# A fused attention and ELU layer: the last block's last two projections batch by batch, and three moves of x given to ScalarE

## The chip, the core and the metric

The kernel runs on one core of one Trainium2 chip. The metric is device time in microseconds (us). Five engines work side by side, each in the order of its own instructions: TensorE (PE, with its weight loads as PEld), VectorE (DVE), ScalarE (ACT), GpSimd (POOL) and SyncE (SP), which here does nothing but issue DMAs. They wait for one another through semaphores.

## What is computed

A linear attention with a decaying state, and then a layer with an ELU between two matrices:

```python
# B, H, S, D = 4, 8, 768, 48 ; d_model = 384, d_ff = 2048
for t in range(S):
    cur = np.einsum('bhd,bhe->bhde', u[None] * kt, vt)
    y[:, :, t] = np.einsum('bhd,bhde->bhe', rt, state + cur)
    state = w[None, :, :, None] * state + np.einsum('bhd,bhe->bhde', kt, vt)
x = y.transpose(0, 2, 1, 3).reshape(B * S, H * D)
h = x @ w_in
g = np.where(h > 0.0, h, np.exp(np.minimum(h, 0.0)) - 1.0)
return g @ w_out
```

The inputs and the result are float32.

## The kernel before

The 768 time steps are cut into six blocks (n = 0 to 5) of 128. A pair (n, b), block and batch, is a unit. A unit's attention gives 128 tokens of x, and the four units of a block stand side by side in x[n], 512 columns wide, kept as a high and a low part whose sum is x (xh and xl), so that each product is made of three matrix products. The layer goes through d_ff in 16 slices (f = 0 to 15). For each (n, f):

- `hidden` (L1171): nine matmuls ps_h <- x, weights, 512 columns, one group of three for each of three 128-row parts c of x;
- `negative` (L1184, ACT, L1188 and L1189), `elu` (L1192, DVE, L1194), `split_g` (L1196: the high part by ACT at L1200, the low part by DVE at L1202);
- `project` (L1205): for each batch b three matmuls of 384 columns that add to ps_acc[b]; they need the two parts of g. It follows two steps behind `hidden`.

After slice 15, `store` (L1221) copies the four sums to `stage`, alternately by ACT (L1231) and DVE (L1229), and SP stores each at once (L1233). The last block has nothing behind it: `run` (L286) does both outstanding projections, f = 14 and f = 15, and then the store.

`fill_x` (L1086) completes x. A unit's eight heads come out as rows of x in four parts, each with 16 rows to spare in both halves, and the fourth part's rows are moved into these spare rows of the other three by six small DMAs, one for each half i and part c (L1098). It is done for batches 0 to 2 at once (384 columns, 48 KB each) and for batch 3 apart (128 columns, 16 KB each). Before block n's first `hidden` can multiply part c, the moves of c in both halves must have landed.

The order is written by hand. `step` (L393) goes through a list of names, `FIRST` for block 0 and `LATER` for the others, and each engine runs its instructions in the order in which they are written there. In `FIRST` the order of the names that matter here is: `hid`, `bk7` (ACT's copy of moved keys, L665, for the unit after), `neg`, `elu`, `gh`, `Gb`, `proj`. `Gb` is `fill_x`; for unit (1, 3) it falls into step (0, 15), the step before block 1's first `hidden`.

Of the kernel before, what the change touches and what calls it, by code (L numbers as in the profile page):

```python
# [17 lines left out]
P = 128  # L18
B, H, S, D = 4, 8, 768, 48
DP = 64  # L20
HP = H // 2
DM, DFF = 384, 2048
NC = DM // P
NF = DFF // P
NCH = S // P
# [8 lines left out]
FILLS = [slice(i * DP + D, (i + 1) * DP) for i in range(2)]  # L34
# [22 lines left out]
class Kernel:  # L57
# [180 lines left out]
    def run_general(self):  # L238
        self.u_by_tokens()
        self.powers_by_tokens()  # L240
        self.reverse_powers()
        self.level_tables()
        self.load_v(0, 1)
        self.load_weights(0)
        self.load_weights(1)
        for n in range(NCH):
            self.all_banks = n == 0
            for b in range(B):
                self.turn_in(n, b)
                self.decay_in(n, b)  # L250
                self.current(n, b)
                self.key_rest(n, b)
                self.scores_by_levels(n, b)
                self.outputs(n, b)
                self.new_state(n, b)
                self.load_after(n, b, self.load_rk)
                self.load_after(n, b, self.load_v)
                for i in range(2):
                    self.split_x(n, b, i)
                self.fill_x(n, b)  # L260
            self.all_banks = False
            for f in range(NF):
                if n == 0:
                    if f == 0:
                        for j in range(2, 2 * DEEP - 1):
                            self.load_weights(j)
                    for k in (0, 1) if f == 0 else (f + 1,):
                        self.widen(k)
                        self.low_bits(k)
                        self.merge(k)  # L270
                        self.sign(k)
                        for j in (2 * k + 2 * DEEP - 1, 2 * k + 2 * DEEP):
                            self.load_weights(j)
                        self.split_w(k)
                        for i in range(2):
                            self.rest_w(k, i)
                self.hidden(n, f)
                self.negative(n, f)
                self.elu(n, f)
                for i in range(2):  # L280
                    self.split_g(n, f, i)
                self.project(n, f)
                if f == NF - 1:
                    self.store(n)

    def run(self):  # L286
        self.start()
        for n in range(NCH):
            for f in range(NF):
                self.step(n, f)  # L290
        for f in (NF - 2, NF - 1):
            self.project(NCH - 1, f)
        self.store(NCH - 1)

    def start(self):
        nc = self.nc
# [96 lines left out]
    def step(self, n, f):  # L393
        nc = self.nc
# [5 lines left out]
        last = divmod(n * NF + f - (1 if (n, f) < EARLY else 2), NF)  # L400
# [49 lines left out]
            "elu": lambda: self.elu(n, f),  # L450
            "gh": lambda: self.split_g(n, f, 0),
            "gl": lambda: self.split_g(n, f, 1),
            "proj": lambda: self.project(*last) if last in self.g else None,
            "Lw": lambda: [self.load_weights(j) for j in (2 * k + 2 * DEEP - 1, 2 * k + 2 * DEEP) if n == 0],
            "wd": lambda: self.widen(k + 1),
            "lb": lambda: self.low_bits(k + 1),
# [14 lines left out]
        if (n, f) == (0, NF - 1):  # L471

            o = self.late.bitcast(F32).rearrange("p s d w -> p (s d w)")[:, 0 : B * DM]
# [612 lines left out]
    def fill_x(self, n, b):  # L1086

        if self.general:
            cols = slice(b * P, (b + 1) * P)
        elif b < HP - 2:  # L1090
            return
        else:
            cols = slice(0 if b == HP - 2 else b * P, (b + 1) * P)
        x = self.x[n].bitcast(F32)[:, :, :, cols]
        for i in range(2):
            for c in range(NC):
                rows = slice(i * DP + c * FILL, i * DP + (c + 1) * FILL)
                self.nc.sync.dma_start(x[FILLS[i], :, c], x[rows, :, NC])  # L1098


    def level_tables(self):
# [100 lines left out]
            nc.vector.tensor_sub(part, g, self.g[n, f][2].bitcast(F32))  # L1202
        self.g[n, f].append(part)

    def project(self, n, f):  # L1205
        gh, gl = self.g.pop((n, f))[2:]
        wh, wl = self.weight(f + 1, 0)
        if f == 0:
            self.acc[n] = [
                self.ps.tile([P, 512], F32, tag=f"acc{b}", name=f"ps_acc{b}", bufs=1)  # L1210
                for b in range(B)
            ]
        for b in range(B):
            at = slice(b * P, (b + 1) * P)
            for i, (a, w) in enumerate(((gh, wh), (gh, wl), (gl, wh))):
                self.nc.tensor.matmul(  # L1216
                    self.acc[n][b][:, 0:DM], lhsT=a[:, at], rhs=w,
                    start=(f == 0 and i == 0), stop=(f == NF - 1 and i == 2),
                )

    def store(self, n):  # L1221
        nc = self.nc
        for b, po in enumerate(self.acc.pop(n)):
            if self.general:
                o = self.wk.tile([P, DM], F32, tag="o", name="o", bufs=2)
            else:
                o = self.o[:, b, :]
            if b % 2:
                nc.vector.tensor_copy(o, po[:, 0:DM])  # L1229
            else:  # L1230
                nc.scalar.copy(o, po[:, 0:DM])  # L1231
            row = b * S + n * P
            nc.sync.dma_start(self.out[row : row + P, :], o)  # L1233
# [43 lines left out]
```

## Time and profile before

| what | us |
|---|---|
| median of 3 runs | 504.34 (504.28 to 504.58) |
| the profiled execution, whole | 505.23 |
| its span, first to last instruction | 503.5 |
| TensorE busy (matmuls) | 487.5, 97% of the span |
| VectorE, ScalarE, GpSimd busy | 284.8, 256.9, 153.6 |

Times within the span are counted from its start, in us. The profiled execution lies 1.73 us above its span and 0.89 us above the median. A row of the timeline gives start, length, engine, line, operation, and in brackets how long the engine stood idle before it and what ended that; "SPq" is a DMA issue on SP's queue. The granted clock (PEclk) is a share of TensorE's full 2.4 GHz.

### The profile page before, as it was taken

To read this page: it belongs to the slowest core of one execution; us is meant where nothing else is said; L and a number is where in the kernel's file an instruction comes from. 1 tells how busy PE (TensorE), PEld (TensorE's weight loads), DVE (VectorE), ACT (ScalarE), POOL (GpSimd) and SP (SyncE) were. 2 spreads that over 40 slices of the span, in tenths; PEclk is the share of its full clock that TensorE was granted. 3 is DMA by queue.
4 is the path that set the end of the run, shared out by engine and by line. 5 is a ranking of instruction groups with operands and counts; after the bars stand their busy time and mean duration, and the time that the engine had idled before them with its cause. 6 is when DMAs were issued, how large, how long until landed. Compare 5 with 4: busy or idle time off the path is not lost.

```text
span 503.5 us, 11963 instructions
## 1 busy us (share of the span) xinstructions
PE 487.5 (97%) x4890; PEld 430.2 (85%) x4890; DVE 284.8 (57%) x501; ACT 256.9 (51%) x449; POOL 153.6 (31%) x169
## 2 busy tenths in 40 slices
PE   8989999999999999999999999999999999999995
PEld 6888887977988988889888888888888989999995
DVE  6989899894565454554454654653654533433331
ACT  2468888863543544544444445445535435444442
POOL 4466769663331322312312303313212201000000
PEclk9999999999999999999999999999999999999999
DMA  9987796834624524624533524444333120100001
GB/s 157 230 184 164 197 182 171 158 92 113 164 61 90 138 61 98 176 61 90 120 79 91 162 61 96 106 77 112 103 108 101 45 65 10 62 1 1 1 0 69
DMA packets 102276, 51.08 MB, mean 101 GB/s; under 512 B 78786, under 2 KB 98116, under 8 KB 102212
## 3 DMA queue, kind: packets, MB, share of 16 engines
q1 hardware_dynamic: 102212, 50.22, 41.7%
q8 instruction: 40, 0.66, 0.6%
q14 instruction: 24, 0.20, 0.2%
HBM read 35.13 MB, written 13.11 MB: 96 GB/s over the span
## 4 chain that ended last, share of the span: by engine, by line
PE 74%; POOL 8%; ACT 4%; DVE 4%; issue 3%; DMA 3%; SPq 1%; ACTq 0%; POOLq 0%; DVEq 0%
PE ps_acc L1216 33%; PE ps_h L1179 32%; POOL wl L612 4%; PE ps_y L985 2%; PE ps_a L907 2%; PE ps_y L993 2%; PE ps_a L921 1%; POOL k_t L735 1%; DMA x<-x 1%; PE ps_y L855 1%; ACT g L1189 1%; ACT g L1188 1%; DMA stage<-in_moe_w_in_dram 1%; ACT x_f L1004 1%; SPq L1098 1%
## 5 line engine op out<-in xcount | busy, mean ns | idle before, releaser
L1216 PE MATMUL ps_acc<-wh,g 128*128 128x384 f32 x768 | 217.0, 343 | 0.4 <-DVE stage L1229 0.2
L1179 PE MATMUL ps_h<-x,wh 128*128 128x512 f32 (+1 forms) x588 | 180.3, 388 | 1.3 <-DMA x<-x 1.3
L1216 PEld LDWEIGHTS ps_acc<-wh,g 128*128 128x128 f32 x768 | 140.1, 188 | 6.2 <-DVE stage L1229 1.3
L1216 PE MATMUL ps_acc<-wl,g 128*128 128x384 f32 x384 | 129.2, 336 | 0.0
L1194 DVE SCALAR_TENSOR_TENSOR ps_h<-g,ps_h 128x512 f32<-128x512 f32 x96 | 66.7, 694 | 103.1 <-ACT g L1189 103.0
L1179 PEld LDWEIGHTS ps_h<-x,wh 128*128 128x128 f32 x588 | 108.1, 188 | 18.2 <-DMA x<-x 1.4
L1179 PE MATMUL ps_h<-x,wl 128*128 128x512 f32 (+1 forms) x294 | 114.8, 391 | 2.6 <-POOL wl L612 2.6
L1188 ACT ACTIVATE g<-ps_h 128x512 f32<-128x512 f32 x96 | 57.6, 600 | 87.5 <-PE ps_h L1179 87.5
L1200 ACT CAST g<-ps_h 128x512 fp32r<-128x512 f32 x96 | 56.3, 587 | 74.6 <-DVE ps_h L1194 74.1
L1202 DVE TENSOR_TENSOR g<-ps_h,g 128x512 fp32r<-128x512 f32 x96 | 66.2, 689 | 45.1 <-ACT g L1200 44.6
L1216 PEld LDWEIGHTS ps_acc<-wl,g 128*128 128x128 f32 x384 | 72.1, 188 | 2.1
L1179 PEld LDWEIGHTS ps_h<-x,wl 128*128 128x128 f32 x294 | 55.2, 188 | 16.0 <-POOL wl L612 4.7
L1189 ACT ACTIVATE g<-g 128x512 f32<-128x512 f32 x96 | 60.7, 632 | 3.1
L735 POOL TENSOR_TENSOR k_t<-k_t,rev 128x384 f32<-128x384 f32 x22 | 24.7, 1123 | 99.4 <-DVE ru L717 92.9
L1022 POOL TENSOR_TENSOR x<-x_f,x 128x512 fp32r<-128x512 f32 x16 | 20.7, 1297 | 90.0 <-ACT x L1020 84.7
L612 POOL TENSOR_TENSOR wl<-wide,wh 128x384 fp32r<-128x384 f32 x29 | 35.9, 1258 | 16.6 <-ACT wh L605 16.6
L969 DVE COPY_PREDICATED a<-mask,ps_a 128x256 f32<-128x256 int32 x40 | 17.7, 444 | 32.3 <-PE ps_a L921 32.3
L1004 ACT COPY x_f<-ps_y 128x256 f32<-128x256 f32 x40 | 12.9, 375 | 43.7 <-PE ps_y L993 43.7
L656 POOL TENSOR_TENSOR rk<-rk,pw 128x512 f32<-128x512 f32 x16 | 19.0, 1190 | 42.2 <-DMA rk<-blocks 42.2
L962 POOL TENSOR_TENSOR a<-ident_h,diag 128x512 f32<-128x512 f32 x20 | 21.6, 1079 | 6.7 <-DVE diag L728 5.3
L1013 DVE TENSOR_TENSOR x_f<-x_f,ps_y 128x128 f32<-128x128 f32 x40 | 9.7, 283 | 22.2 <-ACT x_f L1004 22.2
L587 DVE SCALAR_TENSOR_TENSOR wide<-stage 128x768 int32<-128x768 int32 (+1 forms) x17 | 21.1, 1239 | 0.0
(122 smaller groups left out, 411.0 us busy)
## 6 DMA issues: line engine op xcount, KB each, us to landing
blocks<-tb SPq DMA_DIRECT2D x64, 128.0 KB, 2.3
rk<-blocks SPq DMA_DIRECT2D x16, 512.0 KB, 3.5
stage<-in_moe_w_out_dram SPq DMA_DIRECT2D x16, 384.0 KB, 4.4
stage<-in_moe_w_in_dram SPq DMA_DIRECT2D x32, 144.0 KB, 4.2
out_dram<-stage SPq DMA_DIRECT2D x24, 192.0 KB, 4.2
r_t<-in_r_dram SPq DMA_DIRECT2D x22, 192.0 KB, 4.2
k_t<-in_k_dram SPq DMA_DIRECT2D x22, 192.0 KB, 3.2
v_t<-in_v_dram SPq DMA_DIRECT2D x22, 192.0 KB, 4.9
```

The source lines that it names most:

```text
L587: self.nc.vector.scalar_tensor_tensor(self.place(self.wide, k, WIDE), high, 3, low, op0=ALU.logical_shift_left, op1=ALU.bitwise_or,)
L612: (eng or self.nc.gpsimd).tensor_sub(lo, a, hi.bitcast(F32))
L735: (eng or self.nc.gpsimd).tensor_mul(k, k, self.rev[:, :, 0:D])
L962: self.nc.gpsimd.tensor_mul(un["a"], self.ident_h.unsqueeze(1).to_broadcast([P, H, DP]), un["diag"].unsqueeze(2).to_broadcast([P, H, DP]),)
L1022: (eng or nc.gpsimd).tensor_sub(x[:, 1], xf, x[:, 0].bitcast(F32))
L1179: self.nc.tensor.matmul(ph[:, part], lhsT=a[:, c * P : (c + 1) * P], rhs=x[:, c, part], start=(c == 0 and i == 0), stop=(c == NC - 1 and i ...
L1188: nc.scalar.activation(g, ph, AF.Relu, scale=-1.0)
L1189: nc.scalar.activation(g, g, AF.Exp, scale=-1.0)
L1194: self.nc.vector.scalar_tensor_tensor(ph, g, -1.0, ph, op0=ALU.add, op1=ALU.max)
L1200: nc.scalar.copy(part, g)
L1202: nc.vector.tensor_sub(part, g, self.g[n, f][2].bitcast(F32))
L1216: self.nc.tensor.matmul(self.acc[n][b][:, 0:DM], lhsT=a[:, at], rhs=w, start=(f == 0 and i == 0), stop=(f == NF - 1 and i == 2),)
```

## The change

Two things. Of the six moves of x of unit (1, 3), the three of the half i = 1 are issued on ScalarE's queue and no longer on SP's. And the end of `run` goes batch by batch: f = 14 for batches 0 to 2, then for each batch f = 15 (for batch 3 f = 14 first) with its copy and store right behind it; ACT copies and stores batch 1, DVE and SP batches 0 and 2, and batch 3 is cut into two halves of 192 columns, one by ACT and its queue, one by DVE and SP. The other lines only keep g until both callers have used it.

```diff
         for n in range(NCH):
             for f in range(NF):
                 self.step(n, f)
-        for f in (NF - 2, NF - 1):
-            self.project(NCH - 1, f)
-        self.store(NCH - 1)
+        n, last = NCH - 1, B - 1
+        self.project(n, NF - 2, range(last))
+        for b in range(B):
+            if b == last:
+                self.project(n, NF - 2, (b,))
+            self.project(n, NF - 1, (b,))
+            self.store_last(n, b)
...
-            "proj": lambda: self.project(*last) if last in self.g else None,
+            "proj": lambda: (self.project(*last), self.g.pop(last)) if last in self.g else None,
...
                 rows = slice(i * DP + c * FILL, i * DP + (c + 1) * FILL)
-                self.nc.sync.dma_start(x[FILLS[i], :, c], x[rows, :, NC])
+                queue = self.nc.scalar if (n, b, i) == (1, B - 1, 1) else self.nc.sync
+                queue.dma_start(x[FILLS[i], :, c], x[rows, :, NC])
...
-    def project(self, n, f):
-        gh, gl = self.g.pop((n, f))[2:]
+    def project(self, n, f, batches=range(B)):
+        gh, gl = self.g[n, f][2:]
...
-        for b in range(B):
+        for b in batches:
...
+    def store_last(self, n, b):
+        nc, o, po = self.nc, self.o[:, b, :], self.acc[n][b]
+        row = b * S + n * P
+        cols = (slice(0, DM // 2), slice(DM // 2, DM)) if b + 1 == B else (slice(0, DM),)
+        for i, at in enumerate(cols):
+            if (b + i) % 2:
+                nc.scalar.copy(o[:, at], po[:, at])
+                nc.scalar.dma_start(self.out[row : row + P, at], o[:, at])
+            else:
+                nc.vector.tensor_copy(o[:, at], po[:, at])
+                nc.sync.dma_start(self.out[row : row + P, at], o[:, at])
```

ScalarE, around the step from block 0 to block 1; x_770 is x of block 1, ps_h_1612 the hidden values of (0, 15), ps_h_1652 those of (1, 0). Before:

```order
L1020 CAST x_770<-x_f_1584 128x4x128
L1200 CAST g_0_1595<-ps_h_1527 128x512
L665 COPY tb_1496<-rk_1546 128x512
L1188 ACTIVATE g_1623<-ps_h_1612 128x512
L1189 ACTIVATE g_1623<-g_1623 128x512
L1200 CAST g_0_1627<-ps_h_1612 128x512
L1188 ACTIVATE g_1712<-ps_h_1652 128x512
```

The same place in the changed kernel:

```order
L1025 CAST x_770<-x_f_1584 128x4x128
L1206 CAST g_0_1595<-ps_h_1527 128x512
L670 COPY tb_1496<-rk_1546 128x512
L1194 ACTIVATE g_1623<-ps_h_1612 128x512
L1195 ACTIVATE g_1623<-g_1623 128x512
L1206 CAST g_0_1627<-ps_h_1612 128x512
L1104 DMA x_770<-x_770 16x2x128 x3
L1194 ACTIVATE g_1712<-ps_h_1652 128x512
```

The three moves stand behind the whole activation of (0, 15), and ahead of the first instruction that reads the hidden values of (1, 0). On SP's queue three moves are left where six were.

TensorE, in the last two projections; wh15 and wl15 are the weights of f = 14, wh16 and wl16 those of f = 15, ps_acc0 to ps_acc3 the sums of the four batches. Before:

```order
L1216 MATMUL ps_acc2_5334<-wh15_162,g_1_5714 128x384
L1216 MATMUL ps_acc3_5335<-wh15_162,g_0_5712 128x384
L1216 MATMUL ps_acc3_5335<-wl15_163,g_0_5712 128x384
L1216 MATMUL ps_acc3_5335<-wh15_162,g_1_5714 128x384
L1216 MATMUL ps_acc0_5332<-wh16_164,g_0_5742 128x384
L1216 MATMUL ps_acc0_5332<-wl16_165,g_0_5742 128x384
L1216 MATMUL ps_acc0_5332<-wh16_164,g_1_5744 128x384
```

The same place in the changed kernel:

```order
L1222 MATMUL ps_acc2_5334<-wh15_162,g_1_5714 128x384
L1222 MATMUL ps_acc0_5332<-wh16_164,g_0_5742 128x384
L1222 MATMUL ps_acc0_5332<-wl16_165,g_0_5742 128x384
L1222 MATMUL ps_acc0_5332<-wh16_164,g_1_5744 128x384
L1222 MATMUL ps_acc1_5333<-wh16_164,g_0_5742 128x384
```

The three matmuls of batch 3 for f = 14 have moved from here to ahead of its three for f = 15, which stay the last.

## Rows read from the trace of the kernel before

**Rows 1.** Busy time by stretch: stretch, length, busy of each engine, PEclk, DMA, GB/s.
```profile
100.00:118.00 18.00, 16.18 (x197) 13.61 (x196) 12.78 (x22) 10.83 (x20) 11.23 (x11) 1.00 0.43 117
118.00:130.00 12.00, 12.00 (x175) 10.35 (x176) 7.91 (x17) 5.99 (x12) 3.20 (x4) 1.00 0.41 113
...
200.00:300.00 100.00, 99.74 (x1131) 87.33 (x1132) 54.18 (x105) 46.36 (x85) 25.64 (x26) 1.00 0.41 103
...
400.00:490.00 90.00, 90.00 (x554) 81.44 (x553) 32.07 (x51) 40.63 (x70) 4.18 (x4) 1.00 0.07 22
```

**Rows 2.** Timeline of all engines where block 0 goes over into block 1.
```profile
113.09 3.79 SPq L1098 DMA_DIRECT2D x<-x  x6
...
115.79 0.62 ACT L665 COPY tb<-rk 128x512 f32<-128x512 f32 x1 [2.97 <-DMA rk<-blocks]
...
116.47 0.34 PE L1216 MATMUL ps_acc<-wh,g 128*128 128x384 f32 x1
...
117.60 0.70 DVE L1194 SCALAR_TENSOR_TENSOR ps_h<-g,ps_h 128x512 f32<-128x512 f32 x1 [3.97 <-ACT g L1189]
...
117.90 0.70 PE L1179 MATMUL ps_h<-x,wh 128*128 128x512 f32 x2 [1.09 <-DMA x<-x]
...
118.33 0.59 ACT L1200 CAST g<-ps_h 128x512 fp32r<-128x512 f32 x1 [0.76 <-DVE ps_h L1194]
```

**Rows 3.** The chain that ended last, the same place: start, us, what.
```profile
115.02 0.59 SPq L1098
115.61 0.04 issue
115.65 2.21 DMA x<-x
...
123.58 2.09 PE ps_h L1179 x9
```

**Rows 4.** Line 1098 from 110 to 120 us: lengths of the issues in ns, us to landing.
```profile
L1098 SPq DMA_DIRECT2D x<-x x6: 585/592/602, 113.1 to 116.3; - x6
...
DMA to landing us min/median/max: 2.2/3.1/4.0
```

**Rows 5.** Timeline of PE, 133 to 145 us: its one wait after block 1's start.
```profile
143.52 0.78 PE L985 MATMUL ps_y<-rk,state 48*64 48x64 f32 x14 [0.70 <-DVE mid L931]
```

**Rows 6.** Timeline of all engines at the end.
```profile
494.05 0.69 DVE L1202 TENSOR_TENSOR g<-ps_h,g 128x512 fp32r<-128x512 f32 x1 [0.65 <-ACT g L1200]
...
497.17 0.48 ACT L1231 COPY stage<-ps_acc 128x384 f32<-128x384 f32 x1 [0.56 <-PE ps_acc L1216]
...
497.32 0.34 PE L1216 MATMUL ps_acc<-wh,g 128*128 128x384 f32 x1
497.69 0.56 DVE L1229 COPY stage<-ps_acc 128x384 f32<-128x384 f32 x1 [0.49 <-PE ps_acc L1216]
```

**Rows 7.** The chain's last pieces, the stretch from 488 us on.
```profile
491.36 6.30 PE ps_acc L1216 x36
```

**Rows 8.** Costliest groups of the page: busy, mean ns of one.
```profile
L1004 ACT COPY x_f<-ps_y 128x256 f32<-128x256 f32 x40 | 12.9, 375 | 43.7 <-PE ps_y L993 43.7
L1013 DVE TENSOR_TENSOR x_f<-x_f,ps_y 128x128 f32<-128x128 f32 x40 | 9.7, 283 | 22.2 <-ACT x_f L1004 22.2
```

**Rows 9.** Busy time by quarter microseconds after the last matmul; columns as in Rows 1.
```profile
498.75:499.00 0.25, 0.00 (x0) 0.00 (x0) 0.00 (x0) 0.00 (x0) 0.00 (x0) 1.00 1.15 408
...
500.50:500.75 0.25, 0.00 (x0) 0.00 (x0) 0.00 (x0) 0.00 (x0) 0.00 (x0) 1.00 0.07 25
...
501.50:501.75 0.25, 0.00 (x0) 0.00 (x0) 0.00 (x0) 0.00 (x0) 0.00 (x0) 1.00 0.17 39
501.75:502.00 0.25, 0.00 (x0) 0.00 (x0) 0.00 (x0) 0.00 (x0) 0.00 (x0) 0.50 0.07 25
```

**Rows 10.** SP's store issues: the last two, timeline from 498 us on.
```profile
497.67 1.26 SPq L1233 DMA_DIRECT2D out_dram<-stage  x2
```

More of the change, by code (lines that the diff above doesn't have):

```diff
@@ L282, in run_general @@
                 self.project(n, f)
+                self.g.pop((n, f))
                 if f == NF - 1:
```

## The prediction

> **What bounds the kernel now.** I read busy time by stretches first. From 118 us on TensorE is busy 12.00 of 12.00 us, then 99.74 of 100 between 200 and 300, then 90.00 of 90 from 400 on [rows 1]: it never stops, the other engines are half idle, and whatever delays TensorE by a microsecond after block 0 delays the end by one. Between 100 and 118 us it loses 1.8 of 18 us, and 1.09 of them stand in one row: the first `hidden` of block 1 waits for a move of x [rows 2]. The chain of waits shows which: an SP issue at 115.02, 0.59 us long, then 2.21 us of transfer [rows 3], then TensorE at 117.90 [rows 2]. SP issues the six from 113.09 on, 0.592 us each [rows 2, 4] and about 0.63 from start to start (3.79 us for six), so 115.02 is the fourth: half i = 1, part 0. That fits the code: part 0 needs the first and the fourth move, part 1 the second and fifth, part 2 the third and sixth. After the end of TensorE's work (last matmul 497.32 and 0.34 us long, [rows 6]) come a copy, a store and its landing: DMA traffic goes on to 500.75 [rows 9].
>
> **Part one: three moves go to ScalarE.** On SP nothing bad happens: three issues fewer, 3 x 0.63 = 1.9 us, and the load of r queued behind them starts that much sooner. The moves that stay are the three of i = 0, which land when they did.
>
> The other three are the ones that TensorE waits for, and what counts is when ScalarE reaches them. In its order they stand behind the cast at L1200 of (0, 15) (the `order` rows). They need nothing from it, but ScalarE takes its instructions in order. That cast starts at 118.33 and takes 0.59 us [rows 2], because of a chain that the change leaves alone: ScalarE waits until 115.79 for moved keys (idle 2.97), then L1188 and L1189, then DVE's `elu` from 117.60 to 118.30, then the cast. So the fourth move, on SP at 115.02, is issued by ScalarE at the earliest when the cast is handed over, 118.35, and at the latest when it has ended, 118.95. No row shows a DMA issued by ScalarE. I take the price of the same transfer on SP, 0.59 us of issue, 0.04, 2.21 of landing, and TensorE 0.04 later, 2.88 in all [rows 2, 3]: TensorE starts at 121.2 to 121.8. Without a reason for either end I take the middle, 121.5, against 117.90: **3.6 us later**. The bounds are wider, since the six moves took 2.2 to 4.0 us to land [rows 4]: 118.35 + 2.2 gives 2.7 us later, 118.95 + 4.0 gives 5.0.
>
> The second and third of ScalarE's moves follow at 0.63 us and TensorE's groups of three at 0.7, so they cost no more. What is queued behind the three issues on ScalarE is L1188 of (1, 0), which can't start before TensorE has done that `hidden`, 2.09 us of work [rows 3]; the issues end by 120.9. So these 1.9 us of ScalarE cost nothing; the cover is the very wait they cause.
>
> Does the delay come back? The only later wait of TensorE of that size is 0.70 us at 143.52, for DVE's `mid` [rows 5]; it hangs on DVE work that itself starts from TensorE's results of that unit, so it should move along. I count nothing back and keep 0.7 for the range.
>
> **Part two: the end.** The number of matmuls is the same, 36 in 6.30 us from 491.36 [rows 7], 0.175 each. In the new order f = 15 of batch 0 starts after 12 + 9 of them, 495.04; the high part of g is there since before 494.05, and the low part, ready at 494.74 [rows 6], is needed by the third matmul, at 495.4. That leaves 0.6 us of cover. TensorE ends where it did.
>
> The sums of batches 0 to 2 are complete three matmuls earlier, 0.5 us, and their copies and stores go ahead; they weren't last. Last is batch 3: DVE copies 384 columns in 0.56 us from 497.69 [rows 6]. Now two engines copy 192 columns each. ScalarE takes 0.375 us for 256 columns and 0.48 for 384 [rows 6, 8], so about 0.31 for 192; DVE takes 0.283 us for 128 [rows 8] and 0.56 for 384, so about 0.35. The later of the two ends 0.2 us sooner. The issue behind it may be shorter: SP's last two took 1.26 us together [rows 10], and the move's issues 0.59. And the last store meets less traffic: from 498.75 to 499.00 the queues carried 408 GB/s [rows 9], with several stores under way at once; now the first two or three are out before. Against it: a move of 16 KB still took 2.2 us to land [rows 4], and 500.75 is only 2.5 us after the last copy's end, so the landing of a smaller last store has little to give. Together **0.35 us sooner**; the ends are 0.7 and nothing.
>
> The page "DMA: Bandwidth & Descriptors" of the Trainium skill, section "Issuing engines are not separate DMA queues", says that DMAs of several issuing engines run on the same 16 DMA engines, so that a second issuer saves nothing but issue time. By it the two halves share what one store had, each behind one issue as before; the gain would be the copy's 0.2 alone, and the sum 507.7 instead of 507.6.
>
> **Sum.** On the profiled execution: 505.23 + 3.6 - 0.35 = 508.5; it stands 0.89 us above the median, so 504.34 + 3.25 = **507.6 us**. With the bounds (2.7 to 5.0, less 0.7 for a part made good; 0 to 0.7 at the end) the case alone reaches from 505.6 to 509.3, and most of it lies in 506.6 to 508.6.
>
> **The rivals.**
>
> *The clock falls in the longer gap.* TensorE now stands still from 116.8 to about 121.5, 4.7 us. At the kernel's end it stands still from 497.66 on, and the granted clock is 1.00 until 501.75 and 0.50 after, that is, 1.2 GHz after 4.1 us [rows 9]. So 4.7 us may be enough for `hidden` of (1, 0) to begin at half speed. No row shows how soon the clock comes back. If it does so within that `hidden`, of 2.09 us at full speed [rows 3], up to 2.1 us are lost; nothing if it doesn't fall. I take 1.5: 509.1 us. Against: the gap is only just longer than the one at the end, and 4.4 at its shortest. The page "TensorE: Matmul & The Clock Gate" of the Trainium skill, section "Part 1: The HAM clock gate (the "warmup" mystery)", says the same: an idle array is throttled to half rate and sustained work releases it. The row at the end agrees with the first half; no row here bears on the second.
>
> *Faster: the moves land earlier, as two queues could make them.* If ScalarE issued its three at 113.1 beside SP's, part 0 would land 1.9 us sooner, the wait of 1.09 us would be gone and with the gain at the end the time would be 504.34 - 1.1 - 0.35 = 502.9. It decides at one point: the issue must come before 115.02, and it stands behind a cast that starts at 118.33. Only if ScalarE's queue ran ahead of a waiting instruction could it come true.
>
> *No change.* The delay would have to stay under 1.4 us: an issue at 118.35 that costs nothing beside and lands in 0.9 us, or waits made good later. The quickest of the moves took 2.2. About 504.9.
>
> **Chances.** The forecast 0.60 (506.6 to 508.6 for most of it), the clock 0.27, faster 0.05, no change 0.04; 0.04 is left for something slower still, such as a dearer issue on ScalarE's queue, which no row shows. The range of eight in ten takes the forecast's lower part and most of the clock's: 506.2 to 509.8. A measurement of this kernel tells about 0.2% (1 us) from no change: faster than 503.3 0.05, within 0.04, slower than 505.4 0.91.
>
> **What would show it.** In the changed kernel's profile: three issues of x by ScalarE between 118.3 and 121, the wait of the first `hidden` of block 1 grown from 1.09 to 4.4 to 5.0 us with the same move as its releaser, and all later rows shifted by as much; PEclk 1.00 behind that gap for the forecast, 0.50 for the rival; at the end no wait of TensorE for g, and two short copies. I am wrong if the issues stand before 118, if TensorE doesn't wait at the start of block 1, or if a wait of 3 us or more disappears later.

## The result, and the profile after

The changed kernel took 508.15 us (median of six runs, 506.57 to 509.79) against 504.04 for the kernel before beside it: ratio 1.0085, interval 1.0065 to 1.0106. The forecast was 507.6 in a range of 506.2 to 509.8, slower with a chance of 0.91. The total lies in the range; several of its terms did not come out, so that it is met in part by luck. A second set of runs of the same kernel, in the experiments, gave 506.38 against 504.53 (1.0034, interval 1.0022 to 1.0046). Why two sets of one kernel lie 1.8 us apart is part of what follows.

The profiled run took 507.46 us, its span is 505.7. In the changed kernel the lines have moved: `fill_x` issues at L1104, `hidden` is L1185, `elu` L1200, `split_g` L1206 and L1208, `project` L1222, the new copies of the end are L1233 (ScalarE) and L1236 (VectorE).

First the busy time by stretch, which answers to [rows 1]; the columns are those there.

```profile
100.00:118.00 18.00, 15.98 (x195) 13.40 (x193) 14.15 (x23) 11.04 (x20) 12.54 (x12) 1.00 0.46 120
118.00:130.00 12.00, 11.34 (x164) 9.49 (x165) 5.92 (x13) 3.44 (x8) 1.03 (x1) 0.86 0.26 78
200.00:300.00 100.00, 99.73 (x1076) 87.63 (x1075) 54.18 (x107) 46.36 (x85) 26.16 (x26) 1.00 0.42 105
400.00:490.00 90.00, 90.00 (x554) 81.37 (x553) 32.10 (x51) 41.26 (x72) 4.83 (x4) 1.00 0.08 24
```

The first two lines differ from those of before: TensorE is idle 0.2 and 0.66 us more, and in the second its granted clock (PEclk) is 0.86 where it was 1.00. From 200 us on nothing has changed. So the loss lies where block 0 goes over into block 1, and it is of two kinds, idle time and clock.

The timeline of that place, all engines, answers to [rows 2].

```profile
112.88 1.88 SPq L1104 DMA_DIRECT2D x<-x  x3
...
113.72 0.62 ACT L670 COPY tb<-rk 128x512 f32<-128x512 f32 x1 [1.08 <-DMA rk<-blocks]
...
115.85 0.70 DVE L1200 SCALAR_TENSOR_TENSOR ps_h<-g,ps_h 128x512 f32<-128x512 f32 x1 [2.40 <-ACT g L1195]
...
116.30 0.34 PE L1222 MATMUL ps_acc<-wh,g 128*128 128x384 f32 x1
...
116.58 0.58 ACT L1206 CAST g<-ps_h 128x512 fp32r<-128x512 f32 x1 [0.76 <-DVE ps_h L1200]
116.58 2.00 ACTq L1104 DMA_DIRECT2D x<-x  x3
...
118.66 0.70 PE L1185 MATMUL ps_h<-x,wh 128*128 128x512 f32 x2 [2.03 <-DMA x<-x]
```

SP's three moves go out at 112.88; ScalarE's three go out at 116.58, the very moment at which the cast of (0, 15) starts. TensorE has nothing to do from 116.63 on and waits 2.03 us, where it waited 1.09.

The issues at L1104 from 110 to 125 us (lengths in ns, then first and last start, and the time from issue to landing of all six) answer to [rows 4].

```profile
L1104 ACTq DMA_DIRECT2D x<-x x3: 602/614/718, 116.6 to 118.0; - x3
...
DMA to landing us min/median/max: 1.8/1.8/2.0
```

An issue by ScalarE takes 0.61 us, as one by SP did (0.592), and its transfer lands as soon: 1.8 to 2.0 us behind the issue, quicker than the 2.2 to 4.0 of the profile before; SP's three land as quickly here, so the difference is not the queue's.

The chain of waits there (start, us, what) answers to [rows 3].

```profile
116.58 1.94 DMA x<-x
...
118.66 3.24 PE ps_h L1185 x9
121.90 1.06 PE ps_a L912 x32
```

The first `hidden` of block 1 takes 3.24 us, where nine such matmuls took 2.09 [rows 3], and the 32 small matmuls behind it 1.06. The busy time in single microseconds shows why: the eighth column is the granted clock.

```profile
119.00:120.00 1.00, 1.00 (x6) 0.77 (x5) 0.00 (x0) 0.00 (x0) 0.00 (x0) 0.88 0.09 25
120.00:121.00 1.00, 1.00 (x4) 0.81 (x3) 0.00 (x0) 0.00 (x0) 0.00 (x0) 0.50 0.08 16
...
122.00:123.00 1.00, 1.00 (x44) 1.00 (x48) 0.00 (x0) 0.97 (x2) 0.00 (x0) 0.50 0.00 0
123.00:124.00 1.00, 1.00 (x35) 0.95 (x28) 0.31 (x1) 0.20 (x1) 0.00 (x0) 0.92 0.00 0
```

TensorE started again at 118.66 at full clock; at about 119.8 the clock fell to 1.2 GHz and came back at about 123.2. Summed over these microseconds, 0.12 + 3 x 0.50 + 0.08 = 1.7 us of full-speed work are lost while TensorE never stops. (The microsecond from 121 to 122 is like its neighbours.)

Behind that nothing is given back. TensorE's waits from 119 us to the end, by what it waited for (us in total, times, longest; the first is the wait that ended at 118.66), with only 0.2 us below these:

```profile
PE ps_h L1185 <- DMA x<-x: 2.0, 1, 2.0
PE ps_y L990 <- DVE mid L936: 0.7, 1, 0.7
```

The 0.70 us for `mid` stand where they stood [rows 5].

The end, timeline of all engines, answers to [rows 6].

```profile
499.35 0.34 PE L1222 MATMUL ps_acc<-wh,g 128*128 128x384 f32 x1
499.72 0.32 ACT L1233 COPY stage<-ps_acc 128x192 f32<-128x192 f32 x1 [1.09 <-PE ps_acc L1222]
500.07 0.34 ACTq L1234 DMA_DIRECT2D out_dram<-stage  x1
500.07 0.36 DVE L1236 COPY stage<-ps_acc 128x192 f32<-128x192 f32 x1 [0.84 <-ACT stage L1233]
```

The two half copies don't run side by side: VectorE's begins 0.03 us after ScalarE's has ended, and its idle time names ScalarE. Both read the same tile, the sums of batch 3. TensorE's last 36 matmuls took 6.30 us, as before [rows 7]. The copies end 0.74 us after the last matmul (500.43 against 499.69); the one whole copy before ended 0.59 us after it (498.25 against 497.66, [rows 6]). From the last matmul to the end of the span it is 6.0 us, where it was 5.8.

### The profile page after: what moved, and what is told of

It is laid out like the page before. It is cut to its first block, busy times and chain, and to the rows that moved or that the text cites. A ratio compares the mean times of both kernels' runs of the same rounds, so it can differ in the third digit from the quotient of the medians.

```text
span 505.7 us, 11962 instructions
## 1 busy us (share of the span) xinstructions
PE 489.0 (97%) x4890; PEld 431.4 (85%) x4890; DVE 287.0 (57%) x502; ACT 256.8 (51%) x449; POOL 153.0 (30%) x169
## 4 chain that ended last, share of the span: by engine, by line
PE 79%; POOL 8%; ACT 4%; DVE 4%; issue 3%; DMA 0%; DVEq 0%; ACTq 0%; POOLq 0%
PE ps_acc L1222 34%; PE ps_h L1185 34%; POOL wl L617 4%; PE ps_y L990 2%; PE ps_a L912 2%; PE ps_y L998 2%; PE ps_a L926 1%; POOL k_t L740 1%; ACT g L1195 1%; DVE ps_h L1200 1%; PE ps_y L860 1%; ACT g L1194 1%; POOL state L942 1%; ACT x_f L1009 1%; POOL ru L722 1%
## 5 line engine op out<-in xcount | busy, mean ns | idle before, releaser
L1222 PE MATMUL ps_acc<-wh,g 128*128 128x384 f32 x768 | 216.9, 343 | 0.4 <-DVE stage L1247 0.2
L1185 PE MATMUL ps_h<-x,wh 128*128 128x512 f32 (+1 forms) x588 | 180.8, 389 | 2.0 <-DMA x<-x 2.0
L1222 PEld LDWEIGHTS ps_acc<-wh,g 128*128 128x128 f32 x768 | 140.1, 187 | 6.2 <-DVE stage L1247 1.3
L1222 PE MATMUL ps_acc<-wl,g 128*128 128x384 f32 x384 | 129.1, 336 | 0.0
L1185 PEld LDWEIGHTS ps_h<-x,wh 128*128 128x128 f32 x588 | 108.4, 188 | 19.0 <-issue 2.5
L1200 DVE SCALAR_TENSOR_TENSOR ps_h<-g,ps_h 128x512 f32<-128x512 f32 x96 | 66.6, 694 | 99.3 <-ACT g L1195 99.3
L1185 PE MATMUL ps_h<-x,wl 128*128 128x512 f32 (+1 forms) x294 | 115.3, 392 | 2.5 <-POOL wl L617 2.5
L1206 ACT CAST g<-ps_h 128x512 fp32r<-128x512 f32 x96 | 56.3, 587 | 75.1 <-DVE ps_h L1200 74.7
L1208 DVE TENSOR_TENSOR g<-ps_h,g 128x512 fp32r<-128x512 f32 x96 | 66.2, 689 | 45.5 <-ACT g L1206 45.0
L1222 PEld LDWEIGHTS ps_acc<-wl,g 128*128 128x128 f32 x384 | 72.1, 188 | 2.1
L1185 PEld LDWEIGHTS ps_h<-x,wl 128*128 128x128 f32 x294 | 55.4, 188 | 15.9 <-POOL wl L617 4.4
L592 DVE SCALAR_TENSOR_TENSOR wide<-stage 128x768 int32<-128x768 int32 (+1 forms) x17 | 22.9, 1345 | 0.0
```

The source lines that it names most:

```text
L592: self.nc.vector.scalar_tensor_tensor(self.place(self.wide, k, WIDE), high, 3, low, op0=ALU.logical_shift_left, op1=ALU.bitwise_or,)
L1185: self.nc.tensor.matmul(ph[:, part], lhsT=a[:, c * P : (c + 1) * P], rhs=x[:, c, part], start=(c == 0 and i == 0), stop=(c == NC - 1 and i ...
L1200: self.nc.vector.scalar_tensor_tensor(ph, g, -1.0, ph, op0=ALU.add, op1=ALU.max)
L1206: nc.scalar.copy(part, g)
L1222: self.nc.tensor.matmul(self.acc[n][b][:, 0:DM], lhsT=a[:, at], rhs=w, start=(f == 0 and i == 0), stop=(f == NF - 1 and i == 2),)
```

## The experiments

Theory at the outset: what costs is the place of the three moves in ScalarE's order, behind the cast; the clock's fall is a second cost of the stop that this makes; the end gives a few tenths. Rivals: ScalarE's issue or queue is itself the dear part; the new end costs; or the fall of the clock explains all of it.

One remark for reading mean clocks of single runs. The fall at x takes 1.7 us of 505 off the mean, 0.0034. In every profile the clock falls too some time after the last matmul, where it costs nothing, and takes 0.0003 to 0.0036 off. So a run with a mean of 0.997 or more had no fall at x, one of 0.995 or less had a fall there or elsewhere, and 0.996 can be either. The mean doesn't say where in a run the clock was low; only a profile does.

### The two parts apart

`tail_only` has the new end and leaves all six moves to SP; `moves_only` has the moves and the old end:

```diff
-                self.nc.sync.dma_start(x[FILLS[i], :, c], x[rows, :, NC])
+                queue = self.nc.scalar if (n, b, i) == (1, B - 1, 1) else self.nc.sync
+                queue.dma_start(x[FILLS[i], :, c], x[rows, :, NC])
```

> The new end alone, all six moves of x on SP as before. Theory (the moves cost everything, the end nothing): the two half copies of the last batch stand one behind the other, 0.32 + 0.36 us against 0.56 before, the last store's issue is shorter, and the span ends some 5.8 to 6.0 us after the last matmul as before (5.84): 0.1 us above the kernel before, within 0.3 either way. Rival (the end brings what the prediction took): 0.35 us below. Rival (the end is where the loss came from): 2 us or more above.

> The three moves on ScalarE alone, with the old end. Theory: TensorE waits 2.0 to 3.8 us for x at the first hidden of block 1 instead of 1.1, after that its clock is granted at 0.50 for about 3 us, and the time is 3.9 us above the kernel before, with single runs between 2.3 and 5.7 above. Rival (the end carries part of the loss): less than 3 us above.

The kernel before beside them took 504.47. `tail_only`: 504.67, ratio 1.0006 (0.9998 to 1.0015). `moves_only`: 506.53, ratio 1.0046 (1.0033 to 1.0059). So the moves make the kernel slower, and the end brings nothing; it may cost two tenths. `moves_only` stays 1.8 us under the theory's 3.9, because none of its runs had the fall of the clock.

One line of `tail_only`'s timeline stands for the wait with SP's six moves; the three after it are `moves_only`'s.

```profile
117.97 0.70 PE L1184 MATMUL ps_h<-x,wh 128*128 128x512 f32 x2 [0.27 <-DMA x<-x]
```

```profile
117.46 0.59 ACT L1201 CAST g<-ps_h 128x512 fp32r<-128x512 f32 x1 [0.76 <-DVE ps_h L1195]
117.47 1.99 ACTq L1099 DMA_DIRECT2D x<-x  x3
...
119.53 0.70 PE L1180 MATMUL ps_h<-x,wh 128*128 128x512 f32 x2 [2.01 <-DMA x<-x]
```

With SP the wait is 0.27 us here (0.26 in `tail_whole` below), less than the 1.09 of [rows 2]: in the one profiled execution of the kernel before, the moves landed late, and it was 0.89 us above its own median. Against 0.27 the changed order waits 1.74 us more, and that is most of what `moves_only` costs: in the profile its clock is 1.00 up to the last matmul, none of its five runs has a mean below 0.999, and it is 2.06 us slower.

### The place of the moves

If ScalarE's queue were the dear part, three moves by ScalarE should cost anywhere. `moves_early` puts the same three ahead of ScalarE's copy of the moved keys (a name `Xb` of its own ahead of `bk7` in the list), `early_again` is the same kernel once more, and `moves_mid` puts them behind that copy and ahead of `neg` of (0, 15), that is, ahead of the elu and the cast. All three have the old end.

```diff
-            "G": lambda n, b: self.fill_x(n, b),
+            "G": lambda n, b: self.fill_x(n, b, (0,) if (n, b) == (1, B - 1) else (0, 1)),
+            "X": lambda n, b: self.fill_x(n, b, (1,)) if (n, b) == (1, B - 1) else None,
-... lb hid A9 bk7 kr8 ...
+... lb hid A9 Xb bk7 kr8 ...      (moves_early, early_again)
+... lb hid A9 bk7 Xb kr8 ...      (moves_mid)
...
```

The lines left out let `fill_x` do one half alone and choose the queue as `moves_only` does.

> The three moves on ScalarE, but written ahead of its copy of the moved keys and of the activation of (0, 15), right behind its cast of (0, 14); the old end. Theory (only their place in ScalarE's order costs): ScalarE issues them at 112.9 to 114.8 us, beside SP's three, the wait of 1.1 us at the first hidden of block 1 is gone, and the time is 1.1 us below the kernel before. Rival (an issue on ScalarE's queue is dear in itself, or holds up the activation): the same as the kernel before or above it.

> moves_early once more beside the kernel before: theory, 0.4 to 0.9 us below it again, ratio 0.998 to 0.9995, no fall of the clock. Rival (it was the choice of runs): ratio 0.9995 to 1.001.

> ScalarE's three moves between its copy of the moved keys and the two steps behind it (elu and cast of (0,15)); the old end. Theory (what costs is the chain elu of ScalarE, elu of VectorE, cast that stands between the keys' copy and the moves in the change; the wait for the keys alone costs nothing): the moves are issued 0.6 us behind the start of the copy of the keys, at 114.3 to 114.7, land 1.9 us later while TensorE is still at the projection ahead, and the wait of the first hidden matmul of block 1 is 0.2 to 0.4 us; 503.6 to 504.5, as the kernel before or up to 0.8 below it. Rival (the wait for the keys is enough): issue at 115.5 or later, a wait of 1 us or more and +0.5 to +1.5 us.

`moves_early`: 503.72 against 504.47, ratio 0.9990 (0.9981 to 0.9998). `early_again`: 503.68 against 504.35, ratio 0.9982 (0.9973 to 0.9991). `moves_mid`: 504.01 against 504.35, ratio 0.9993 (0.9984 to 1.0002). Timeline of `moves_early`:

```profile
113.15 1.87 SPq L1100 DMA_DIRECT2D x<-x  x3
113.15 2.16 ACTq L1100 DMA_DIRECT2D x<-x  x3
...
117.11 0.73 PE L1181 MATMUL ps_h<-x,wh 128*128 128x512 f32 x2 [0.20 <-DMA x<-x]
```

And of `moves_mid`:

```profile
113.60 0.62 ACT L666 COPY tb<-rk 128x512 f32<-128x512 f32 x1 [0.99 <-DMA rk<-blocks]
113.63 2.04 ACTq L1100 DMA_DIRECT2D x<-x  x3
...
116.43 0.63 PE L1181 MATMUL ps_h<-x,wh 128*128 128x512 f32 x2
```

Same queue, same three issues, and no cost: ScalarE's queue is not the dear part. In `moves_mid` the issues begin 0.03 us after the copy of the keys has begun and the first `hidden` starts without a wait (a weight load for its last part waits 0.55 us, which sets the matmuls back by 0.27). So the wait for the keys alone costs little, against the rival there; what costs is the chain elu, cast behind it, some 3 us. Three moves early on a second queue even gain 0.7 us over SP's six, where 1.1 was expected: the issues of both engines begin together at 113.15 instead of one behind the other over 3.79 us.

The landings differ from one profiled execution to the next, and profiles must be compared with that in mind. In ten of the fourteen a move lands 1.8 to 2.2 us after its issue, in `moves_mid` 1.8 to 3.0; in the kernel before it takes 2.2 to 4.0, in `moves_early` 3.2 to 3.9 and in `early_whole` below 3.3 to 4.0. In these three the moved keys are late too: GpSimd starts on them at 115.6 to 116.2 us, elsewhere at 113.7 to 114.9. From the end of one `project` to the start of the next, with the first `hidden` of block 1 between, 4.42 us pass in the kernel before and 3.57 in `moves_early` (late landings), 3.58 in `tail_only` and 3.06 in `early_again` (quick ones). So the early moves gain 0.85 or 0.52 us there, like against like, and the 0.7 of the medians lies between. The 0.84 us between 4.42 and 3.58 also come close to the 0.89 by which the profiled run of the kernel before lies above its median. What makes landings late in an execution stays open.

### The fall of the clock

`after_again` is the changed kernel itself, `moves_again` is `moves_only`, both on one chip with the kernel before.

> The changed kernel once more, to see how its single runs spread. Theory: the wait for x at the first hidden matmul of block 1 grows to about 2.0 us in every run, which costs 2.1 to 2.4 us; in a part of the runs the granted clock falls to 1.2 GHz behind that wait and costs 2 to 3 us more, so that the runs stand in two groups: mean granted clock 0.996 or above at +2.1 to +2.5 us over the kernel before, and below that at +3.5 to +5. Median between +2.2 and +4.5. Rival (moves and new end cost about 2 us more together than apart, whatever the clock): all runs at +3.5 or more, also those whose clock is 0.999.

> ScalarE's three moves alone, with the old end, beside the changed kernel on the same chip. Theory (the fall of the clock is a matter of the run, not of the new end): again +2.0 to +2.4 us without a fall, and falls in some runs here too, at +4 to +5. Rival (only the whole change brings the fall): no run with a mean clock below 0.998, all at +1.8 to +2.8.

The kernel before: 504.53. `after_again`: 506.38, ratio 1.0034 (1.0022 to 1.0046); its six runs with a mean clock of 0.997 or more lie from 505.93 to 506.98, the one at 0.994 took 508.08. `moves_again`: 506.83, ratio 1.0041 (1.0027 to 1.0056); four of its twelve runs have 0.994 or less, 506.83 to 509.38. The profiled run of `after_again` has no fall, that of `moves_again` has one. First line the restart of TensorE, second the microsecond behind 120; of `after_again`:

```profile
119.34 0.70 PE L1185 MATMUL ps_h<-x,wh 128*128 128x512 f32 x2 [2.03 <-DMA x<-x]
...
120.00:121.00 1.00, 1.00 (x6) 0.85 (x5) 0.00 (x0) 0.00 (x0) 0.00 (x0) 1.00 0.07 19
```

And of `moves_again`:

```profile
118.91 0.70 PE L1180 MATMUL ps_h<-x,wh 128*128 128x512 f32 x2 [2.02 <-DMA x<-x]
...
120.00:121.00 1.00, 1.00 (x4) 0.78 (x3) 0.00 (x0) 0.00 (x0) 0.00 (x0) 0.56 0.02 8
```

The stop is the same to a hundredth of a microsecond, and once the clock falls and once it doesn't. That gives the price of the fall in time that passes: from its restart TensorE needs 4.84 us to the next `project` in the first profile of the changed kernel (118.66 to 123.50) and 4.86 in `moves_again`, but 3.35 in `after_again` and 3.31 in `moves_only`: 1.5 us. The rival of `moves_again` (only the whole change brings the fall) is wrong, and so is that of `after_again`: runs of the whole change without a fall stand at +1.4 to +2.5 us, 1.7 by their median, and the moves alone at +2.06 (`moves_only`) and +1.6 (`moves_again`, its six runs at 0.997 or more) by theirs. In the first set of the changed kernel five of six runs had the fall (0.990 to 0.994: 507.46 to 509.79) and one had not (0.999: 506.57). That is the difference between the two sets, as far as the clock explains it: the five lie 0.9 to 3.2 us above the one, and the run at 0.990 lost more of its clock than one such fall and the longest end seen take together (0.0070), which no profile caught. Runs without a fall differ as well: those of `moves_again` reach 507.70, above two of its four with one. The Trainium skill, page "TensorE: Matmul & The Clock Gate", section "Part 1: The HAM clock gate (the "warmup" mystery)", says that the monitor behind the gate runs on without regard to the start of a kernel, so that the same kernel can meet it at another point in each run; the two profiles agree with it, and no run tests it. What made five of six in one set and one of nine in the other stays open.

Two kernels fill the stop with matmuls that nobody reads, ahead of the first `hidden` of block 1: `moves_warm` has the moves, the old end and 4 calls, `after_warm` the whole change and 16:

```diff
-            "hid": lambda: self.hidden(n, f, self.rest_of(n, f)),
+            "hid": lambda: (
+                self.keep_warm(16) if (n, f) == (1, 0) else None, self.hidden(n, f, self.rest_of(n, f))
+            ),
```

> The three moves on ScalarE, the old end, and four more matmuls of the identity (about 2 us of TensorE's time, into a bank that nothing reads) just ahead of the first hidden of block 1, in the wait. Theory (the clock that falls behind the wait costs 1.5 us or more): the clock stays at 1.00 from 117 to 126 us, the nine matmuls of that hidden take 2.1 us and not 3.2, and the time is 1.6 us below moves_only. Rival (the wait alone costs, and the low clock is made good later): the same as moves_only.

> The changed kernel with 16 more 128-column matmuls, about 2.1 us of work whose result nobody reads, on TensorE just ahead of the first hidden matmul of block 1, where it would wait for x. Theory (the stop for x is what the clock falls behind): no run with a fall there, mean clock 0.998 or above, +2.3 to +2.6 us over the kernel before with a small spread. Rival (the fall has another cause): runs at clock 0.995 and below and +3.5 to +5 us as in the changed kernel.

`moves_warm` was 506.14 against 504.47, ratio 1.0046 (1.0029 to 1.0064). The extra matmuls took only 1.05 us and left a stop of 1.13; six of its eight runs lie from 505.55 to 506.2 at 0.997 and more, two at 508.48 and 508.82 with 0.996 and 0.993. A shorter stop still has falls: one by its clock, a second, to judge by its time. The 1.6 us below `moves_only` that the theory gave didn't come (the two ratios are the same), since `moves_only` had no fall to be spared. `after_warm` was 507.73 against 504.53, ratio 1.0058 (1.0043 to 1.0074). Its extra matmuls took 3.73 us, longer than the stop: the first `hidden` begins at 120.45 instead of 119.34, and these 1.1 us are most of the 1.35 by which it is slower than `after_again`; the theory, with 2.1 us of matmuls, had +2.3 to +2.6 and not +3.2. No run of its six is below 0.996. With one fall in nine in `after_again` this doesn't prove that filling the stop prevents the fall; it fits.

`moves_late` makes the stop longer: eight copies by ScalarE that nobody reads, ahead of its moves, which stand as in `moves_only`.

```diff
+                if (n, b, i) == (1, B - 1, 1) and c == 0:
+                    for _ in range(8):
+                        self.nc.scalar.copy(self.spare, self.ident)
```

> ScalarE's three moves where the change has them, behind eight more copies of 128x128 by ScalarE that nobody reads; the old end. Theory A (the stop of TensorE sets only how likely the clock falls): the moves start some 1.8 to 2.2 us later than in moves_only, the wait is 3.8 to 4.2 us, the runs whose clock holds are at +3.8 to +4.4 us over the kernel before, and the clock falls in most runs, at +5.5 to +7. Rival B (the fall is a matter of the run alone): falls in a quarter to a third of the runs, as with the 2 us stop.

It was 510.97 against 504.35, ratio 1.0138 (1.0122 to 1.0153). Timeline and clock of its profiled run:

```profile
119.99 2.29 ACTq L1103 DMA_DIRECT2D x<-x  x3
...
122.06 1.19 PE L1184 MATMUL ps_h<-x,wh 128*128 128x512 f32 x2 [4.81 <-DMA x<-x]
...
121.00:122.00 1.00, 0.00 (x0) 0.00 (x0) 0.00 (x0) 0.00 (x0) 0.00 (x0) 0.80 0.06 16
```

The copies took 2.61 us, more than the 1.8 to 2.2 put down, and the stop was 4.81 us. Here the clock fell before TensorE started again. All four runs had the fall (three have 0.990 or 0.991, the fourth is the profiled one): four of four, against ten of 32 with a stop of 2 us, if 0.996 is counted as no fall. That fits theory A, by which a longer stop makes the fall likelier. But `moves_late` ran on another chip than `moves_only`, `after_again` and `moves_again`, so that a difference of chips isn't ruled out.

### The end

`tail_whole` keeps the end batch by batch, but copies each batch whole (VectorE 0 and 2, ScalarE 1 and 3) and lets SP issue all stores; the moves are as before. `early_whole` joins that end to the early moves.

```diff
+        if b % 2:
+            nc.scalar.copy(o, po[:, 0:DM])
+        else:
+            nc.vector.tensor_copy(o, po[:, 0:DM])
+        nc.sync.dma_start(self.out[row : row + P, :], o)
```

> ScalarE's three moves ahead of its copy of the moved keys, as in moves_early, and the last two projections batch by batch with whole copies (two by VectorE, two by ScalarE) and all stores by SP. Theory: 0.75 us below the kernel before from the moves (moves_early) and about 0.4 from the shorter end, so some 1.1 below. Rival (what follows the last jump sets the end, not the copies and stores): as moves_early, 0.6 to 0.9 below.

> The last two projections batch by batch with whole copies (two by VectorE, two by ScalarE), all stores by SP, the moves as in the kernel before. Theory (VectorE, ScalarE and SP each jump once at the end, and their jumps take 3.5 us or more when all three fall within 0.8 us, as with two half copies, and about 2.9 when they stand apart): the branches stand about 1 us apart, SP's first instruction behind its branch comes 2.7 to 3.0 us after it, the span ends 5.4 to 5.7 us after TensorE, and the time is 0.1 to 0.4 us below the kernel before. Rival (batch by batch itself costs): 0.2 above, as tail_only.

`tail_whole`: 503.83 against 504.35, ratio 0.9996 (0.9987 to 1.0005). `early_whole`: 504.09 against 504.53, ratio 0.9990 (0.9979 to 1.0001), not better than `moves_early`; the 0.4 us that the theory gave to the end did not come. Neither interval is clear of no change.

Behind the kernel's body each engine jumps out of a branch and then runs a short common end. For each engine the next lines give the branch (the last start is that at the end) and the first instruction behind it (first start). Of the kernel before:

```profile
L1243 DVEq COMPARE_BRANCH  x2: 50/54/57, 5.5 to 497.7; - x2
L1243 SPq COMPARE_BRANCH  x2: 46/48/49, 6.1 to 499.0; - x2
...
L1272 SPq EVENT_SEMAPHORE  x10: 17/28/28, 501.9 to 503.4; - x10
L1272 DVEq DRAIN  x2: 10/34/58, 501.0 to 503.0; - x2
```

Of the changed kernel:

```profile
L1261 ACTq COMPARE_BRANCH  x2: 42/44/45, 5.2 to 500.4; - x2
L1261 DVEq COMPARE_BRANCH  x2: 50/54/57, 5.5 to 500.1; - x2
L1261 SPq COMPARE_BRANCH  x2: 46/48/49, 6.1 to 500.8; - x2
...
L1290 SPq EVENT_SEMAPHORE  x10: 17/28/28, 504.4 to 505.7; - x10
L1290 DVEq DRAIN  x2: 10/34/58, 504.1 to 505.3; - x2
L1290 ACTq DRAIN  x2: 8/44/80, 504.2 to 505.2; - x2
```

Of `tail_whole`:

```profile
L1257 DVEq COMPARE_BRANCH  x2: 50/54/57, 5.5 to 495.9; - x2
L1257 SPq COMPARE_BRANCH  x2: 46/48/49, 6.0 to 497.9; - x2
...
L1286 SPq EVENT_SEMAPHORE  x10: 17/28/28, 500.4 to 501.7; - x10
L1286 DVEq DRAIN  x2: 10/34/57, 498.8 to 501.3; - x2
```

The branch takes 0.05 us; the next instruction of SP comes 2.9 us later in the kernel before, 3.6 in the changed one, 2.6 in `tail_whole`. SP's branch stands 1.3 us behind the last matmul before and 1.1 in the changed kernel, so the new end does reach it 0.2 us sooner than in that profile (in three others with the old end it stands at 1.0), and loses 0.7 behind it. In the changed kernel the three engines jump within 0.8 us of one another and all take 3.6 to 4.0; in the two kernels with whole copies the jumps are about 1 us apart and take 2.6 to 3.0. With the old end SP takes 2.6 to 3.0, and 3.5 once (`moves_warm`).

Behind its branch SP asks for the landing of one DMA after another. Whether the last store holds it up there, SP's waits of the kernel before tell:

```profile
SPq L1272 <- DMA out_dram<-stage: 0.3, 1, 0.3
```

The last store there lands at 502.5, 4.2 us after its issue, when SP has stood at this row of waits since 501.9, and the span's end is 0.3 us later for it. In the changed kernel the half stores land at 503.7 and 503.9, before SP comes to ask at 504.4, and SP waits for none; nor does it in `tail_whole`. In `early_whole` it waits 0.5 us. From the last matmul to the end of the span it is 6.0 to 6.1 us in the four profiles with half copies, 5.3 to 5.9 in the eight with the old end, and 4.8 (`tail_whole`, for which the theory had 5.4 to 5.7) and 5.6 with whole copies. That the engines hinder one another in loading what they jump to is one reading, and only argued: DMA queues of the kind "instruction" move packets in this stretch, but as many (6 on queue 14) in the kernel before. That the stores' own packets, which run until 503.4 in the changed kernel, delay the loading is another. No run separates the two. What is measured is that the end with half copies isn't shorter.

## Why the prediction was right, and where it was not

**TensorE sets the time and gives nothing back: right.** After 119 us it waits for `mid` 0.7 us as before, and nothing was made good.

**The moves wait behind the cast: right in mechanism, and nearly twice too dear.** The releaser, the place and the engine are as forecast; `moves_early` and `moves_mid` show that it is the place and not the queue. Two signs that the prediction named came out against it, all the same: issues before 118 were to show it wrong, and they stand at 116.58, behind the cast, which came early; and the wait was to grow to 4.4 us or more, and grew to 2.03. The forecast of +3.6 us was a start of TensorE at 121.5 after a stop of 4.7 us; measured were 118.66 and 2.0, and the cost without the clock is 1.6 to 2.1 us by medians of runs. Three terms were mis-sized, by 0.8, 0.3 and 1.75 us. The landing was taken as 2.88 us in all and is 2.08 (116.58 to 118.66). The issue was put half-way between the cast's start and its end; it goes out with its start, the lower end, 0.3 us sooner. And the cast itself stood at 118.33 in the one profile of before because the keys came late there (copy at 115.79, [rows 2]). In the changed kernel and in `tail_only`, `moves_only`, `after_again`, `moves_again` and `moves_late`, none of which moves that load, the copy starts from 113.72 to 114.84 and the cast from 116.58 to 117.64, 0.7 to 1.75 us sooner. The same execution had SP's moves landing late, a wait of 1.09 that is 0.27 in `tail_only`. A sum on one execution inherits what was unusual in it, on both sides of the difference; that this one stood 0.89 us above the median was seen, but the 3.6 us worked out on it were carried over to the median whole.

**The clock: a rival with a chance of 0.27 that came true in most runs of the first set.** Its price was put at 1.5 us, and 1.5 us pass in the profiles (1.7 us of full-speed work). Its condition was wrong: the clock at the kernel's end had fallen 4.1 us after TensorE stopped [rows 9], and I took a stop of that length to be needed. It fell behind a stop of 2.0 us, after TensorE had worked again for over 1 us. The same look at the changed kernel's own end would have warned: there it falls about 2.4 us after the last matmul, and in the fourteen profiles 1.9 to 5.2 us after it. One falling edge in one profile isn't a threshold.

**The end: -0.35 forecast, nothing to +0.2 measured.** Two assumptions failed. The halves run one behind the other (0.84 us of VectorE's idle time put down to ScalarE), so the copy ends 0.15 us later instead of 0.2 sooner. And what sets the end was misread. DMA traffic doesn't end at 500.75: [rows 9] itself shows 39 GB/s at 501.50, and the last store landed at 502.5. The smaller last store did have something to give; its landing comes 4.2 us behind the last matmul instead of 4.8 in these two profiles. But SP's first instruction behind its branch comes 0.7 us later than before, so that SP finds the landing done and gains nothing by it.

**The sum.** 507.6 was met by 508.15 because the move's share, about 1.6 us too high, stood for a fall of the clock that wasn't in it. Against the second set, 506.38, the forecast is 1.2 us too high, and that is the mis-sized wait less the gain at the end that didn't come. So two errors made each other good in the first set. The case that I called likeliest, a stop of 4.7 us with the clock at 1.00 behind it, was seen in no profile.

**Faster, and no change: rightly given little.** The faster rival named its own condition, an issue before 115.02, and `moves_early` shows what it is worth when that holds: 0.7 us, not 1.1, since the wait to be won is smaller than in the one profile (0.27 in `tail_only`).

## What to carry to other kernels

A DMA that is given to a second engine takes its place in that engine's order: before moving it, look up what the engine waits for just ahead of that place and when the transfer is needed. The same three issues cost 2 us behind a cast and gain 0.7 us ahead of the copy of the keys, so a new queue is worth trying at several places of the order, not at one. For a sum of a few microseconds read the starting times in more than one profile where they are to be had, and where a stop of TensorE grows, as here to 2 us, count a fall of its clock as a case with a price of its own, not as an addition to long stops only.

The version that beats both kernels is the one with ScalarE's moves ahead of its copy of the keys and the old end: 503.68 us against 504.35, and 503.72 against 504.47.

## What the runs showed of the hardware that I had not expected

- ScalarE issues a DMA while it still executes the instruction ahead: the first issue stands at 116.58 with the cast of 0.58 us (at 113.63 beside a copy from 113.60 in `moves_mid`). In `moves_late`, with eight copies ahead, which run from 117.68 for 2.61 us, to 120.29, the first issue stands at 119.99.
- The granted clock can fall after TensorE has restarted: at 119.8, when it had worked again since 118.66, behind a stop of 2.0 us; it came back at 123.2, with TensorE busy all the time. With the same stop it held in other runs.
- VectorE's and ScalarE's copies out of one sum, of different columns into different columns, were run one behind the other (0.84 us of idle time). The program itself has VectorE wait for ScalarE there, though no column is shared; whether the chip could run the two side by side was not tried.
- At the end a branch of 0.05 us is followed by 2.6 to 4.2 us until the next instruction of VectorE, ScalarE or SP; VectorE and ScalarE take longest (3.6 to 4.2) where the three jump within 0.8 us.
- By ScalarE's queue a move of 16 KB within the on-chip memory lands as soon as by SP's in the same profile: 1.8 to 2.0 us by both in the changed kernel, 3.2 to 3.9 by both in `moves_early`.
